# First expert of a routed layer: five residuals on the vector engine, dispatch of both batches merged and placed ahead of the next weight splits, loads issued 20 products earlier

## The chip, the core and the metric

One core of a Trainium2 chip runs the whole program. Its engines work side by side: PE multiplies matrices into PSUM (PEld is its weight load), DVE (the vector engine) and ACT (the scalar engine) do elementwise work, POOL (GpSimd) does elementwise work on SBUF and issues indirect DMAs, SP issues plain DMAs. Each engine has a list of instructions of its own and goes through it in order; an instruction that needs another engine's result waits on a semaphore, and all behind it in that list wait too. The metric is the time of one execution in microseconds (us).

## What is computed

Three stages follow each other: an attention with local windows and global tokens, a feed-forward layer with three input matrices, and a layer of eight routed experts. The change lies in the third:

```python
def _moe2_ref(x, w_gate, w1, w2, capacity) -> np.ndarray:      # x: 1088 x 512, w1: 8 x 512 x 1024, w2: 8 x 1024 x 512
    logits = x @ w_gate
    expert_idx = np.argmax(logits, axis=1)
    ...
    for i in range(N):
        e = expert_idx[i]
        if counts[e] < capacity:
            disp[e, counts[e]] = x[i]
            pos[i] = counts[e]
            counts[e] += 1
            keep[i] = True
    h = np.maximum(np.einsum('ecd,edf->ecf', disp, w1), 0.0)
    y = np.einsum('ecf,efd->ecd', h, w2)
    ...
        if keep[i]:
            out[i] = gate_w[i] * y[expert_idx[i], pos[i]]
```

The capacity is 288 rows per expert, and tokens take their places in order, batch 0 first (544 rows), then batch 1.

## The kernel before

**Matmuls in pairs of halves.** Every float32 factor is split into a rounded high part and a low part, the residual (high subtracted from the whole). A product is the sum of three: high by high, high by low, low by high. So each chunk of an expert's weights (128 x 1024 floats, 512 KB) goes through `split(j, k)`: ACT casts it to the high part, and another engine subtracts to get the residual. `residuals_on` says which engine: POOL for chunks (0, 6), (0, 7), (1, 0), (1, 1), (1, 3) and for two chunks of each later expert, else DVE. (j, k) means chunk k of the j-th expert to run; chunks 0 to 3 hold w1 (`w1h`, `w1l`), 4 to 7 hold w2 (`w2h`, `w2l`). Raw chunks lie in a ring of five buffers (`rawb`); `split` also issues on SP the load of the chunk five further on, into the buffer that it empties.

**The order by products.** The kernel writes the program's order by hand. `drive(main, sides)` steps through a main generator that yields once per matmul ("product"), and after each product runs the side generators that are due; a side yields the number of products to let pass. For the first expert (called j = 0; it holds the full 288 rows that batch 0 alone gives it) the main chain is `first_wide` (products 1 to 96: eight blocks f0 to f7 of 12 products each, one PSUM bank a block, evicted by ACT and DVE into `hhl`, the hidden activations), then `second` for rows 0 to 127 (97 to 120), for rows 128 to 255 (121 to 144) and `second_few` for the last 32 rows (145 to 160). Its sides are `final`/`finish` (routing and dispatch, below), the rows of the last feed-forward window (`tail_rows`), loads, the splits of chunks (0, 5) to (0, 7), the eight splits of expert 1 (`prepare`), and the transposes of expert 1's gathered tokens (`tokens`, tiles `xg` to `xT`).

**Routing and dispatch.** While the first expert runs, the program still has to route batch 1. `final` does: `tail_logits(3)` and `route` (on DVE: argmax, gate, one-hot rows `oh_all`; then `pp` on PE, counts by a triangular matmul; then the place of each token in its expert, and `wvr`, the rank of the experts); `columns` (five DVE instructions on 5 numbers per partition) and `rows_1` (a one-hot matrix of 5 blocks by 128) for a batch of five 128-row blocks; `values` (the other factor, 5 blocks by 24 columns by 5 values); `hand_over` (the matmuls `pd`, which scatter token numbers, output rows and gates to the expert lists); `place_rows` (the lists `idsall`) and `order` (which expert runs when). Then `start` issues three gathers of expert 1's tokens on POOL. The number of products between these steps are Y0 to Y4. Before the change, columns, rows and values run for batch 0 (blocks 0 to 4), then for batch 1 (blocks 5 to 9).

Expert 1 follows in tiles of 128 rows (`first_tile`, `second`), then experts 2, 3 and 4 of the sorted order, one tile each; the others have no rows.

Of the kernel before, what the change touches and what calls it, by code (L numbers as in the profile page):

```python
# [7 lines left out]
F32 = mybir.dt.float32  # L8
# [11 lines left out]
P = 128  # L20
# [6 lines left out]
NE = 8  # L27
# [17 lines left out]
def tile_block(ctx: ExitStack, tc: tile.TileContext, qk, qg, v, vo, vg, w123, w_out, w_gate, w1, w2, consts, out):  # L45
# [389 lines left out]
    def route(b0, b1, pool, tag, wait):  # L435
# [35 lines left out]
        pos = rt.tile([P, nb], F32, name=f"rp{b0}")  # L471
        nc.vector.tensor_reduce(pos, t, axis=AX.X, op=ALU.add)
        POS[b0] = (pos, code)
        return pp[:, nb]

    POS = {}

    def columns(b0, nb):

        pos, _ = POS[b0]  # L480
        t = rt.tile([P, 2, nb], F32, tag="pct", name="pct")
        pm = rt.tile([P, nb], BF16, tag="pcm", name="pcm")
        nc.vector.tensor_scalar(t[:, 0], pos, float(P), None, op0=ALU.is_ge)
        nc.vector.scalar_tensor_tensor(t[:, 0], pos, 2.0 * P, t[:, 0], op0=ALU.is_ge, op1=ALU.add)
        nc.vector.scalar_tensor_tensor(pm, t[:, 0], float(-P), pos, op0=ALU.mult, op1=ALU.add)

        nc.vector.tensor_scalar(t[:, 1], pos, float(CAP), NONE, op0=ALU.is_ge, op1=ALU.mult)
        nc.vector.tensor_tensor(t[:, 0], t[:, 0], t[:, 1], op=ALU.add)
        return t[:, 0], pm
# [232 lines left out]
    def tail_logits(wi):  # L722

        c0, T, x2T, pl_, logits = TAIL[wi]
        lt = XB[wi][2]
        if wi < 3:
            logits(3)
            nc.vector.tensor_copy(lt[:, :T], pl_[0:16, :T])
        yield 8
        ptl = ps_y.tile([P, 4, NE], F32, tag="py", name=f"ptl{c0}")  # L730
        for i, (c, n, row, blk) in enumerate(rows_of(wi)):
            nc.tensor.matmul(ptl[0:n, i], lhsT=lt[:, c - c0 : c - c0 + n], rhs=dup8, start=True, stop=True)
        for i, (c, n, row, blk) in enumerate(rows_of(wi)):
            nc.vector.tensor_copy(L[0:n, blk], ptl[0:n, i])
# [256 lines left out]
    def early():  # L991
# [18 lines left out]
        col, pm = columns(0, 5)  # L1010
# [3 lines left out]
        values(Bv, 0, 5, col, wv0, 3)  # L1014
        yield 44
# [78 lines left out]
    Y0, Y1, Y2, Y3, Y4 = 8, 12, 14, 14, 10  # L1094

    def final():

        yield from tail_logits(3)
        c_ = yield from route(5, 10, ps_mm, "mm", 32)
# [4 lines left out]
        sc = pB.tile([P, 512], F32, tag="hs", bufs=2, name="sc")  # L1104
        g_, p_ = (sc[:, 64 * i : 64 * i + 64].rearrange("p (a b) -> p a b", a=NE) for i in range(2))
# [183 lines left out]
```

## Time and profile before

| | before |
|---|---|
| median of 3 runs | 386.12 us (383.12 to 386.4) |
| the profiled execution | 382.62 us, of which the span from first to last instruction is 380.8 us |
| PE busy | 331.3 us (87%) |
| DVE / ACT / POOL busy | 256.2 (67%) / 178.5 (47%) / 168.6 us (44%) |
| mean DMA rate | 159 GB/s |
| mean granted TensorE clock | 0.968 of full |
| the first expert's block on PE | 252.17 to 299.74 us of the span |

The rows further down come from the profile of that one execution; times are us from the start of the span. A timeline row gives start, length (of the whole group when it ends in "xN"), engine, line, operation, output <- input, shape, and in brackets the idle time of that engine just before and what ended it. Matmul lengths overlap, so the pace of PE is read from one start to the next.

### The profile page before, as it was taken

The page shows a single profiled execution, that of the slowest core. Times are in us where ns is not written, and L with a number is a line of the kernel's source. Part 1 is how long each engine was busy: PE and PEld are TensorE (multiplying, and loading weights), DVE is VectorE, ACT ScalarE, POOL GpSimd, SP SyncE. Part 2 cuts the span into 40 slices and gives each one's busy share as a digit, 9 for nine tenths or more (in the row PEclk, how much of TensorE's full clock was granted, in tenths as well). Part 3 has the DMA queues.
Part 4 walks back from the last instruction along what each step waited for, and adds up shares of the span by engine and source line. Part 5 has one row for each costly group of instructions (what it writes and reads, how often), then busy time and mean ns, then how long its engine had stood idle before and what let it go on. Part 6 is the DMA issues. An engine that isn't in the chain of part 4 may idle for free. (4 is left out here: it accounts for less than half of the span.)

```text
span 380.8 us, 8527 instructions
## 1 busy us (share of the span) xinstructions
PE 331.3 (87%) x3115; PEld 274.3 (72%) x3115; DVE 256.2 (67%) x649; ACT 178.5 (47%) x452; POOL 168.6 (44%) x172
## 2 busy tenths in 40 slices
PE   7988789999999999966899989999249899876892
PEld 2444557777888999966799979989247688655681
DVE  2679989858782698999953385658982661566450
ACT  3876568666642323233222124535504662756640
POOL 0268686646582464574640004000935571353421
PEclk9999989999999999999999999999959999998998
DMA  7964865905297132331000237417646673398500
GB/s 270 406 246 163 297 229 205 344 26 166 74 244 157 57 100 68 112 97 69 2 0 6 107 124 275 127 58 256 197 155 200 213 283 135 95 306 279 192 22 10
DMA packets 26216, 60.67 MB, mean 159 GB/s; under 512 B 3003, under 2 KB 8123, under 8 KB 26160
## 3 DMA queue, kind: packets, MB, share of 16 engines
q1 hardware_dynamic: 24640, 55.69, 44.3%
q0 software_dynamic: 1520, 4.28, 3.1%
q8 instruction: 30, 0.49, 0.5%
q14 instruction: 26, 0.21, 0.2%
HBM read 55.61 MB, written 7.47 MB: 166 GB/s over the span
## 5 line engine op out<-in xcount | busy, mean ns | idle before, releaser
L422 PE MATMUL h<-xh,wh 128*128 128x256 f32 (+1 forms) x288 | 86.0, 299 | 8.0 <-DVE hA L408 6.8
L422 PE MATMUL h<-xl,wh 128*128 128x256 f32 (+1 forms) x288 | 85.1, 296 | 0.0
L422 PE MATMUL h<-xh,wl 128*128 128x256 f32 (+1 forms) x288 | 84.7, 294 | 0.0
L422 PEld LDWEIGHTS h<-xh,wh 128*128 128x128 f32 x288 | 55.4, 192 | 10.3 <-DVE hA L408 8.3
L422 PEld LDWEIGHTS h<-xl,wh 128*128 128x128 f32 x288 | 55.5, 193 | 0.9 <-issue 0.7
L422 PEld LDWEIGHTS h<-xh,wl 128*128 128x128 f32 x288 | 55.5, 193 | 0.3 <-issue 0.2
L412 POOL TENSOR_TENSOR hTl<-hA,hTh 128x288 fp32r<-128x288 f32 (+1 forms) x18 | 15.5, 861 | 57.1 <-ACT hTh L410 57.0
L827 DVE TENSOR_TENSOR w2l<-rawb,w2h 128x1024 fp32r<-128x1024 f32 x14 | 21.4, 1532 | 22.3 <-ACT w2h L826 22.3
L923 PE MATMUL py<-w2h,hhl 128*128 128x512 f32 x112 | 31.0, 406 | 0.2 <-ACT hhl L911 0.2
L224 POOL CAST xh<-xs 128x128 fp32r<-128x128 f32 x32 | 13.7, 428 | 36.7 <-ACT xs L222 36.7
L321 POOL TENSOR_TENSOR ct<-ct,wh 128x512 f32<-128x512 f32 x18 | 25.7, 1429 | 7.5 <-DVE ca L318 5.7
L827 POOL TENSOR_TENSOR w2l<-rawb,w2h 128x1024 fp32r<-128x1024 f32 x5 | 13.1, 2633 | 34.2 <-DVE ab L505 31.3
L702 PE MATMUL x<-hTh,wo_h 128*128 128x256 f32 (+1 forms) x96 | 28.1, 293 | 0.1
L889 PE MATMUL ph<-w1h,xT 128*128 128x512 f32 x80 | 22.2, 411 | 6.8 <-ACT w2h L826 4.3
L702 PE MATMUL x<-hTl,wo_h 128*128 128x256 f32 (+1 forms) x96 | 28.0, 292 | 0.0
L186 ACT ACTIVATE sm<-sm,nm 128x128 f32<-128x128 f32 x64 | 25.2, 399 | 5.5 <-DVE nm L181 5.4
L702 PE MATMUL x<-hTh,wo_l 128*128 128x256 f32 (+1 forms) x96 | 27.8, 289 | 0.0
L408 DVE TENSOR_TENSOR hA<-hA,h 128x256 f32<-128x256 f32 (+1 forms) x48 | 20.7, 432 | 8.5 <-PE h L422 6.8
L322 POOL TENSOR_TENSOR wl<-ct,ca 128x512 fp32r<-128x512 f32 x18 | 24.0, 1335 | 3.5 <-DVE ca L320 2.3
L923 PEld LDWEIGHTS py<-w2h,hhl 128*128 128x128 f32 x112 | 21.7, 195 | 5.3 <-ACT hhl L911 0.6
L410 ACT CAST hTh<-hA 128x256 fp32r<-128x256 f32 (+1 forms) x24 | 10.1, 419 | 32.1 <-DVE hA L408 32.1
L305 DVE TENSOR_SCALAR ca<-ca 128x512 f32<-128x512 f32 x24 | 23.5, 978 | 1.2 <-ACT ca L303 1.1
(205 smaller groups left out, 793.9 us busy)
## 6 DMA issues: line engine op xcount, KB each, us to landing
rawb<-in_w_dram SPq DMA_DIRECT2D x40, 512.0 KB, 4.3
raww<-in_w_dram SPq DMA_DIRECT2D x18, 512.0 KB, 4.5
rawv<-in_v_dram SPq DMA_DIRECT2D x16, 512.0 KB, 5.7
qk<-in_qk_dram SPq DMA_DIRECT2D x16, 320.0 KB, 6.4
rawo<-in_w_out_dram SPq DMA_DIRECT2D x6, 512.0 KB, 3.6
rw<-in_w_dram SPq DMA_DIRECT2D x5, 512.0 KB, 3.7
out_dram<-zero SPq DMA_DIRECT2D x1, 2176.0 KB, 15.9
rawg<-in_vo_dram SPq DMA_DIRECT2D x4, 512.0 KB, 6.6
```

The source lines that it names most:

```text
L186: nc.scalar.activation(sm[:, j], sm[:, j], AF.Exp, bias=nm[:, j : j + 1], scale=-1.0, accum_out=ssum[:, j : j + 1])
L224: nc.gpsimd.tensor_copy(dst[0], xs)
L305: nc.vector.tensor_scalar(a.bitcast(F32), a.bitcast(F32), F64_LO, F64_HI, op0=ALU.max, op1=ALU.min)
L321: nc.gpsimd.tensor_tensor(tf, tf, hi.bitcast(F32), op=ALU.subtract)
L322: nc.gpsimd.tensor_tensor(lo, tf, a.bitcast(F32), op=ALU.add)
L408: nc.vector.tensor_tensor(hA[:, :T], hA[:, :T], ph[:, :T], op=ALU.max)
L412: eng.tensor_tensor(hl[:, f_, c0 : c0 + T], hA[:, :T], dst.bitcast(F32), op=ALU.subtract)
L422: nc.tensor.matmul(ph[:, :T], lhsT=w_[:, a], rhs=x_[:, c, c0 : c0 + T], start=n == 0, stop=n == 11)
L702: nc.tensor.matmul(po[:, :T], lhsT=w_[:, f, d * P : (d + 1) * P], rhs=h_[:, f_, c0 : c0 + T], start=k == 0, stop=k == 17)
L827: residuals_on(j, k).tensor_tensor(l_, raw_of(j, k), h_.bitcast(F32), op=ALU.subtract)
L889: nc.tensor.matmul(ph[0:nt], lhsT=a[:, c], rhs=w_[:, c, sl], start=i == 0, stop=i == 11)
L923: nc.tensor.matmul(py[0:nt], lhsT=a[:, c, a0 : a0 + nt], rhs=w_[:, c], start=i == 0, stop=i == 23)
```

## The change

- `residuals_on`: the five residuals of the first two experts that POOL did go to DVE; those of later experts stay.
- `columns` now writes into `pos_all` and `col_all`, arrays for all ten blocks; `values` runs once over ten blocks (its five steps on twice the columns, the last one as two instructions of five blocks).
- `final`: columns and rows of batch 0 run at the very start, before batch 1's logits; `pp` comes after 24 products instead of 32; columns and rows of batch 1, then the merged values; then a long pause (44 products) up to `pd`.
- Sides: loads at product 36 instead of 56; split (0, 5) at 3 instead of 66, (0, 6) at 72, (0, 7) at 80; the splits of expert 1 at 116 to 160 instead of 85 to 158. In `early` (dispatch of the first expert alone) a pause grows from 44 to 60 products.

```diff
     def residuals_on(j, k):
-        return nc.gpsimd if (j, k) in ((0, 6), (0, 7), (1, 0), (1, 1), (1, 3)) or j > 1 and k in (2, 6) else nc.vector
+        return nc.gpsimd if j > 1 and k in (2, 6) else nc.vector
...
-    def values(Bv, b0, nb, col, wv, ncol):
+    def values(Bs, oq, nb, wv, ncol):
...
-        nc.vector.scalar_tensor_tensor(qb, q, NONE, col, op0=ALU.add, op1=ALU.add)
-        oq = rt.tile([P, 5, 3 * NE], BF16, tag="voq", name="voq")[:, 0:nb, 0:ncol]
+        nc.vector.scalar_tensor_tensor(qb, q, NONE, col_all[:, 0:nb], op0=ALU.add, op1=ALU.add)
         nc.vector.tensor_tensor(oq, iota_b[:, 0:ncol].unsqueeze(1).to_broadcast([P, nb, ncol]), qb.unsqueeze(2).to_broadcast([P, nb, ncol]), op=ALU.is_equal)
-        nc.vector.tensor_tensor(
-            Bv, oq.unsqueeze(3).to_broadcast([P, nb, ncol, NV]),
-            val_all[:, b0 : b0 + nb].unsqueeze(2).to_broadcast([P, nb, ncol, NV]), op=ALU.mult)
+        for i, Bv in enumerate(Bs):
+            b = slice(5 * i, 5 * i + 5)
+            nc.vector.tensor_tensor(
+                Bv, oq[:, b].unsqueeze(3).to_broadcast([P, 5, ncol, NV]),
+                val_all[:, b].unsqueeze(2).to_broadcast([P, 5, ncol, NV]), op=ALU.mult)
...
-    Y0, Y1, Y2, Y3, Y4 = 8, 12, 14, 14, 10
+    Y0, Y1, Y2, Y3, Y4 = 10, 12, 44, 12, 3
 
     def final():
 
+        hs_ = [pB.tile([P, 512], F32, tag="hs", bufs=2, name=f"sc{i}") for i in range(2)]
+        As = [t.bitcast(BF16)[:, 256:896].rearrange("p (b m) -> p b m", b=5) for t in hs_]
+        rows_1(As[0], columns(0, 5), 5)
         yield from tail_logits(3)
-        c_ = yield from route(5, 10, ps_mm, "mm", 32)
+        c_ = yield from route(5, 10, ps_mm, "mm", 24)
...
         yield Y0
...
-        for i in range(2):
-            col, pm = columns(5 * i, 5)
-            rows_1(As[i], pm, 5)
-            yield Y1
-            values(Bs[i], 5 * i, 5, col, wvr, 3 * NE)
-            yield Y2
+        rows_1(As[1], columns(5, 5), 5)
+        yield Y1
...
+        values(Bs, hs_[1].bitcast(BF16)[:, 0 : NBLK * 3 * NE].rearrange("p (b c) -> p b c", b=NBLK), NBLK, wvr, 3 * NE)
+        yield Y2
         pd = ps_y.tile([P, 3 * NE * NV], F32, tag="py", name="pd")
...
-            [finish(), later(6, tail_rows(3)), loads(56, (0, 6), (0, 7), (1, 0), (1, 1)), splits(0, [(5, 66), (6, 72), (7, 69)]), prepare(1, (85, 97, 112, 101, 125, 129, 135, 158)), tokens(1, (149, 154, 163))],
+            [finish(), later(6, tail_rows(3)), loads(36, (0, 6), (0, 7), (1, 0), (1, 1)), splits(0, [(5, 3), (6, 72), (7, 80)]), prepare(1, (116, 120, 124, 130, 138, 146, 152, 160)), tokens(1, (149, 154, 163))],
```

**How it moves instructions.** On POOL, at the start of the first expert's block (behind the branch), before the change; `w2l` and `w1l` are the residuals, `out_dram<-y` the scatter of a result tile, `xg<-x2d` the gathers of expert 1's tokens:

```order
L1177 COMPARE_AND_BRANCH
L827 TENSOR_TENSOR w2l_3551<-rawb,w2h_3550 128x1024 x2
L827 TENSOR_TENSOR w1l_3861<-rawb,w1h_3860 128x1024 x3
L930 DMA out_dram<-y,ids_3091 1088x512
L785 DMA xg_3544<-x2d,idsall 128x512
L785 DMA xg_3545<-x2d,idsall 128x512
L785 DMA xg_3546<-x2d,idsall 32x512
L930 DMA out_dram<-y,ids_3091 1088x512
```

and the same place after the change:

```order
L1175 COMPARE_AND_BRANCH
L785 DMA xg_3545<-x2d,idsall 128x512
L785 DMA xg_3546<-x2d,idsall 128x512
L785 DMA xg_3547<-x2d,idsall 32x512
L930 DMA out_dram<-y,ids_3093 1088x512 x2
```

POOL has no residual left in this block, and the three gathers stand ahead of both scatters.

On DVE, at the start of the same block, after the change (before the change the row behind the branch was the copy to `L`, of batch 1's logits `ptl`):

```order
L1175 COMPARE_AND_BRANCH
L482 TENSOR_SCALAR pct<-pos_all 128x5
L483 SCALAR_TENSOR_TENSOR pct<-pos_all,pct 128x5
L484 SCALAR_TENSOR_TENSOR pcm<-pct,pos_all 128x5
L486 TENSOR_SCALAR col_all<-pos_all 128x5
L487 TENSOR_TENSOR col_all<-col_all,pct 128x5
L492 TENSOR_TENSOR sc_3872<-iota_b,pcm 128x640
L827 TENSOR_TENSOR w2l_3552<-rawb,w2h_3551 128x1024
L734 COPY L<-ptl_3900 32x8
```

Columns and rows of batch 0 and the residual of chunk (0, 5) now stand in front of the routing.

On DVE, in the middle of the block, around the eviction of block f4 (rows L873 and L875 are one block's eviction of the low part of `hhl`), before the change, from batch 0's rows to f5's eviction:

```order
L493 TENSOR_TENSOR sc<-iota_b,pcm 128x640
L873 SCALAR_TENSOR_TENSOR hhl<-ph,hhl 128x256
L875 SCALAR_TENSOR_TENSOR hhl<-ph,hhl 128x32
L498 TENSOR_TENSOR vt<-oh_all,wvr 128x40
L500 TENSOR_REDUCE vq<-vt 128x5
L502 SCALAR_TENSOR_TENSOR vqb<-vq,pct 128x5
L504 TENSOR_TENSOR voq<-iota_b,vqb 128x120
L505 TENSOR_TENSOR ab_4008<-voq,val_all 128x600
L827 TENSOR_TENSOR w2l_3551<-rawb,w2h_3550 128x1024
L873 SCALAR_TENSOR_TENSOR hhl<-ph,hhl 128x256
```

and after the change, from f3's eviction to f5's:

```order
L873 SCALAR_TENSOR_TENSOR hhl<-ph,hhl 128x256
L875 SCALAR_TENSOR_TENSOR hhl<-ph,hhl 128x32
L497 TENSOR_TENSOR vt<-oh_all,wvr 128x80
L499 TENSOR_REDUCE vq<-vt 128x10
L501 SCALAR_TENSOR_TENSOR vqb<-vq,col_all 128x10
L502 TENSOR_TENSOR sc_3873<-iota_b,vqb 128x240
L505 TENSOR_TENSOR ab_4038<-sc_3873,val_all 128x600
L505 TENSOR_TENSOR ab_4039<-sc_3873,val_all 128x600
L873 SCALAR_TENSOR_TENSOR hhl<-ph,hhl 128x256
L875 SCALAR_TENSOR_TENSOR hhl<-ph,hhl 128x32
L873 SCALAR_TENSOR_TENSOR hhl<-ph,hhl 128x256
```

The merged values now stand ahead of f4's eviction, where before they stood behind it. PE's block f6 writes into the PSUM bank that f4's eviction empties: there are three banks for f0, f1, f2, f4, f5 and f6, and one of the three holds `pp` until the end of `final`.

## Rows read from the trace of the kernel before

**Rows 1.** Timeline of PE, the end of the hidden layer to the second.

```profile
263.86 1.39 PE L868 MATMUL ph<-xT,w1h 128*128 128x288 f32 x8
...
268.90 0.44 PE L511 MATMUL pd<-ab,sc 128*128 128x120 bf16 x5
280.95 0.66 PE L511 MATMUL pd<-ab,sc 128*128 128x120 bf16 x5 [11.62 <-DVE ab L505]
...
282.81 2.98 PE L923 MATMUL py<-w2h,hhl 128*128 128x512 f32 x8
285.62 1.08 PE L923 MATMUL py<-w2l,hhl 128*128 128x512 f32 x4
286.54 1.99 PE L923 MATMUL py<-w2h,hhl 128*128 128x512 f32 x8
```

**Rows 2.** Timeline of DVE in that wait, dispatch of batch 1.

```profile
267.50 1.95 DVE L483 TENSOR_SCALAR pct<-rp 128x5 f32<-128x5 f32 x1
...
277.44 1.90 DVE L498 TENSOR_TENSOR vt<-oh_all,wvr 128x40 f32<-128x40 bf16 x1
```

**Rows 3.** Timeline of POOL, residuals and the first gather.

```profile
266.02 5.70 POOL L827 TENSOR_TENSOR w2l<-rawb,w2h 128x1024 fp32r<-128x1024 f32 x2 [31.25 <-DVE ab L505]
271.68 7.60 POOL L827 TENSOR_TENSOR w1l<-rawb,w1h 128x1024 fp32r<-128x1024 f32 x3
...
289.95 1.51 POOL L785 DMA_INDIRECT xg<-x2d,idsall  x1 [0.30 <-issue]
```

**Rows 4.** Windows: busy us (instructions) of PE, PEld, DVE, ACT, POOL; clock; DMA.

```profile
278.00:281.00 3.00, 0.05 (x1) 0.04 (x1) 2.86 (x6) 0.00 (x0) 1.28 (x1) 0.50 0.47 154
```

**Rows 5.** Timeline of PE, the end of the first expert.

```profile
292.89 0.63 PE L951 MATMUL pyf<-w2h,hhl 128*64 128x512 f32 x2
...
294.80 0.66 PE L797 MATMUL xp<-cst,xg 128*128 128x128 f32 x4 [0.35 <-DMA xg<-x2d,idsall]
...
297.64 0.66 PE L797 MATMUL xp<-cst,xg 128*128 128x128 f32 x4 [1.04 <-DMA xg<-x2d,idsall]
...
299.74 1.19 PE L889 MATMUL ph<-w1h,xT 128*128 128x512 f32 x4
```

**Rows 6.** Timeline of DVE, routing and dispatch of batch 0.

```profile
254.77 0.30 DVE L734 COPY L<-ptl 32x8 f32<-32x8 f32 x3 [1.97 <-PE ptl L732]
...
259.87 0.42 DVE L873 SCALAR_TENSOR_TENSOR hhl<-ph,hhl 128x256 fp32r<-128x256 f32 x1 [1.22 <-ACT hhl L872]
...
260.37 0.20 DVE L470 TENSOR_TENSOR rt<-oh_all,pp 128x40 f32<-128x40 bf16 x1
...
262.33 0.16 DVE L483 TENSOR_SCALAR pct<-rp 128x5 f32<-128x5 f32 x1
...
263.82 0.42 DVE L873 SCALAR_TENSOR_TENSOR hhl<-ph,hhl 128x256 fp32r<-128x256 f32 x1
...
264.26 0.19 DVE L498 TENSOR_TENSOR vt<-oh_all,wvr 128x40 f32<-128x40 bf16 x1
...
265.23 0.78 DVE L505 TENSOR_TENSOR ab<-voq,val_all 128x600 bf16<-128x600 bf16 x1
265.93 1.22 DVE L827 TENSOR_TENSOR w2l<-rawb,w2h 128x1024 fp32r<-128x1024 f32 x1
```

**Rows 7.** Timeline of PE, two earlier stalls in the feed-forward layer.

```profile
166.42 0.39 PE L422 MATMUL h<-xh,wh 128*128 128x256 f32 x1 [2.10 <-DVE hA L408]
...
178.75 0.39 PE L422 MATMUL h<-xh,wh 128*128 128x256 f32 x1 [2.62 <-DVE hA L408]
```

**Rows 8.** Windows, columns as in rows 4, behind the second of these stalls.

```profile
180.00:182.00 2.00, 2.00 (x11) 2.00 (x11) 1.93 (x3) 0.16 (x1) 2.00 (x2) 0.50 0.00 0
```

**Rows 9.** Timeline of ACT, expert 1's first tile.

```profile
304.94 0.59 ACT L911 CAST hhl<-hp 128x512 fp32r<-128x512 f32 x1 [0.20 <-PE hp L910]
```

**Rows 10.** DMA issues of 255 to 300 us: KB each, median us to landing.

```profile
rawb<-in_w_dram SPq DMA_DIRECT2D x14, 512.0 KB, 4.0
...
xg<-x2d,idsall POOLq DMA_INDIRECT x5, 4.8
```

More of the change, by code (lines that the diff above doesn't have):

```diff
@@ L470, in route @@
         nc.vector.tensor_tensor(t, oh, pp[:, 0:nb], op=ALU.mult)
-        pos = rt.tile([P, nb], F32, name=f"rp{b0}")
-        nc.vector.tensor_reduce(pos, t, axis=AX.X, op=ALU.add)
-        POS[b0] = (pos, code)
+        nc.vector.tensor_reduce(pos_all[:, b0:b1], t, axis=AX.X, op=ALU.add)
         return pp[:, nb]
-    POS = {}
+    pos_all = rt.tile([P, NBLK], F32, name="pos_all")
+    col_all = rt.tile([P, NBLK], F32, name="col_all")
     def columns(b0, nb):
-        pos, _ = POS[b0]
-        t = rt.tile([P, 2, nb], F32, tag="pct", name="pct")
+        pos, col = pos_all[:, b0 : b0 + nb], col_all[:, b0 : b0 + nb]
+        t = rt.tile([P, nb], F32, tag="pct", name="pct")
         pm = rt.tile([P, nb], BF16, tag="pcm", name="pcm")
[L483 to L489, printed above, removed]
+        nc.vector.tensor_scalar(t, pos, float(P), None, op0=ALU.is_ge)
+        nc.vector.scalar_tensor_tensor(t, pos, 2.0 * P, t, op0=ALU.is_ge, op1=ALU.add)
+        nc.vector.scalar_tensor_tensor(pm, t, float(-P), pos, op0=ALU.mult, op1=ALU.add)
+        nc.vector.tensor_scalar(col, pos, float(CAP), NONE, op0=ALU.is_ge, op1=ALU.mult)
+        nc.vector.tensor_tensor(col, col, t, op=ALU.add)
+        return pm
     def rows_1(A, pm, nb):
         nc.vector.tensor_tensor(A, iota_b.unsqueeze(1).to_broadcast([P, nb, P]), pm.unsqueeze(2).to_broadcast([P, nb, P]), op=ALU.is_equal)
-    def values(Bv, b0, nb, col, wv, ncol):
-        t = rt.tile([P, nb, NE], F32, tag="rt", name="vt")
-        nc.vector.tensor_tensor(t, oh_all[:, b0 : b0 + nb], wv.unsqueeze(1).to_broadcast([P, nb, NE]), op=ALU.mult)
+    def values(Bs, oq, nb, wv, ncol):
+        t = rt.tile([P, nb, NE], F32, tag="vt", name="vt")
+        nc.vector.tensor_tensor(t, oh_all[:, 0:nb], wv.unsqueeze(1).to_broadcast([P, nb, NE]), op=ALU.mult)
         q = rt.tile([P, nb], F32, tag="vq", name="vq")
@@ L1009, in early @@
         nc.vector.tensor_scalar(wv0, mine[:, 0], -NONE, None, op0=ALU.mult)
-        col, pm = columns(0, 5)
+        pm = columns(0, 5)
         A = s2b.tile([P, 5, P], BF16, tag="pA0", bufs=1, name="pA0")
@@ L1013, in early @@
         Bv = s2b.tile([P, 5, 3, NV], BF16, tag="pB0", bufs=1, name="pB0")
-        values(Bv, 0, 5, col, wv0, 3)
-        yield 44
+        values([Bv], s2b.tile([P, 5, 3], BF16, tag="oq0", bufs=1, name="oq0"), 5, wv0, 3)
+        yield 60
         pd = ps_y.tile([P, 3 * NV], F32, tag="py", name="pd0")
@@ L1103, in final @@
             nc.vector.scalar_tensor_tensor(k_, mine[:, i], big, k_, op0=ALU.mult, op1=ALU.add)
-        sc = pB.tile([P, 512], F32, tag="hs", bufs=2, name="sc")
-        g_, p_ = (sc[:, 64 * i : 64 * i + 64].rearrange("p (a b) -> p a b", a=NE) for i in range(2))
+        g_, p_ = (hs_[0][:, 64 * i : 64 * i + 64].rearrange("p (a b) -> p a b", a=NE) for i in range(2))
         nc.vector.tensor_tensor(g_, k_.unsqueeze(1).to_broadcast([P, NE, NE]), k_.unsqueeze(2).to_broadcast([P, NE, NE]), op=ALU.is_gt)
@@ L1110, in final @@
         yield Y0
-        ab = [pB.tile([P, 512], F32, tag="y", bufs=2, name=f"ab{i}").bitcast(BF16) for i in range(2)]
-        As = [sc.bitcast(BF16)[:, 256:896].rearrange("p (b m) -> p b m", b=5), pB.tile([P, 512], F32, tag="hs", bufs=2, name="sc2").bitcast(BF16)[:, 0:640].rearrange("p (b m) -> p b m", b=5)]
-        Bs = [t[:, 0 : 5 * 3 * NE * NV].rearrange("p (b c v) -> p b c v", b=5, v=NV) for t in ab]
-        for i in range(2):
-            col, pm = columns(5 * i, 5)
-            rows_1(As[i], pm, 5)
-            yield Y1
-            values(Bs[i], 5 * i, 5, col, wvr, 3 * NE)
-            yield Y2
+        rows_1(As[1], columns(5, 5), 5)
+        yield Y1
+        Bs = [pB.tile([P, 512], F32, tag="y", bufs=2, name=f"ab{i}").bitcast(BF16)[:, 0 : 5 * 3 * NE * NV].rearrange("p (b c v) -> p b c v", b=5, v=NV) for i in range(2)]
+        values(Bs, hs_[1].bitcast(BF16)[:, 0 : NBLK * 3 * NE].rearrange("p (b c) -> p b c", b=NBLK), NBLK, wvr, 3 * NE)
+        yield Y2
         pd = ps_y.tile([P, 3 * NE * NV], F32, tag="py", name="pd")
```

## The prediction

> **What bounds the kernel now.** I read PE's timeline first. PE is the busiest engine, so time is won or lost where it stands still. In the first expert's block it does so once for long: the five matmuls of `pd` for batch 0 run at 268.90, those for batch 1 only at 280.95, after 11.62 us idle for DVE's `ab` [rows 1]. This wait is dispatch, not weights: every later matmul of this expert is queued behind `pd` in PE's order.
>
> Then DVE in that stretch. Batch 1's columns, rows and values are small instructions, but those on 5 numbers take about 2 us: six rows from 267.50 to 277.44 last 1.90 to 2.27 us [rows 2]. The same column step of batch 0 took 0.16 at 262.33 [rows 6]. What differs is POOL: it subtracts five residuals from 266.02 to 279.28, 2.5 to 2.9 us each [rows 3], and the slow steps lie wholly inside. Larger DVE steps there keep their lengths; a small step seems to be held until a POOL instruction ends.
>
> The stall costs more than its length. TensorE's granted clock is down to 0.50 (1.2 GHz) at 278 to 281 [rows 4], and after the restart eight matmuls that take 1.8 us at full pace (four take 0.92, from 285.62 to 286.54) need 2.81 [rows 1]. At full pace 285.62 would come 3.1 us after 268.90 (ten `pd` 0.6, eleven matmuls at 0.23), so at 272.0: 13.6 us lost, 11.6 stall and 2.0 slow clock. Last, the end of the first expert: from 292.89 to 299.74 there are 16 matmuls (3.65) and three groups of transposes (1.0), 4.65 us of work in 6.85 [rows 5]. PE waits for the gathered tokens: the first gather is issued at 289.95 [rows 3] and lands 4.8 us later [rows 10]. That is 2.2 us more.
>
> **What the change takes away.** With no residuals on POOL in this block, batch 1's small steps should take 0.16 to 0.2 us, and the merged values stand some 40 products ahead of `pd`. So the stall of 11.6, the slow restart of 2.0 and, because the gathers go out earlier (below), the 2.2 of token waits can all go: 15.8 us.
>
> **What it adds: DVE is late for f6.** PE's f6 needs the bank that DVE empties with f4's eviction. Before, that eviction began at 263.82 [rows 6] and f6 started about 264.4, in the middle of the eight matmuls of 263.86, hardly delayed [rows 1]. Now much DVE work stands in front:
> - At the block's start columns and rows of batch 0 take 1.49 (262.33 to 263.82, rows 6) and the residual of (0, 5) 1.14 to 1.22. DVE idled 1.97 before 254.77 [rows 6], so the copy to `L` slips by 0.7 us, by 1.2 if the branch costs DVE half a us (no row shows that). The whole routing slips with it.
> - `pp` needs f0's bank, whose eviction on DVE slips too: PE waits there 0.2 to 0.7 us at product 33. On the other hand `pp` comes eight products sooner, and DVE's idle 1.22 before 259.87 [rows 6] is used.
> - So the step after `pp`, at 260.37 before, comes at 259.5 to 259.9. From there: routing's end 1.53, f2's eviction 0.43 (together 260.37 to 262.33), columns and rows of batch 1 1.49, f3's eviction 0.44, merged values 2.5 (batch 0's took 1.67 from 264.26 to 265.93; doubled columns add about 0.1, a second 600-column step 0.70), f4's eviction 0.52. Sum 6.9: f4's bank is free at 266.4 to 266.8, against 264.3 when PE would want it.
>
> So PE stands 2.1 to 2.6 us at f6, the wait at `pp` included: I take 2.4. Nothing hides it. Behind f6 the eviction of f4 to f7 and two residuals follow on DVE, done by about 271.0, and the second layer needs the last of them some 4 us later.
>
> **The clock at f6.** A stall of 2.10 us at 166.42 was followed by matmuls at full pace; after one of 2.62 at 178.75 [rows 7] the clock was 0.50 [rows 8]. Ours lies between. A fall would cost at most the 2.0 us seen above; I leave it out of the sum, at a chance of a third.
>
> **The five residuals on DVE.** 1.14 to 1.22 each there against 2.5 on POOL. (0, 6) and (0, 7) fill DVE while PE stands or runs f6 and f7. Expert 1's eight residuals (9.8 us) run from about 272 to 289, paced by ACT's casts, which now wait behind the eviction of the first result tile (product 120, about 276.2). w1's four residuals are ready near 282, PE wants them at 286.4: covered by 4 us. What follows is expert 2's loads: each waits for a residual that frees its buffer. Chunk (2, 2) would load at about 285 and land 4.0 later [rows 10], or up to 2 later when loads queue. ACT's cast of it stands ahead of `hhl` in the first tile, at 304.94 before, 5.2 after the tile's start [rows 9]; now 291.6. So 0 to 1.2 us may be lost; I take 0.6.
>
> **The gathers.** `pd` now runs at about 270.9, the lists are ready near 272.1, and POOL issues three gathers in 1.0 to 1.5 us each [rows 3], ahead of both scatters. They land at about 278 to 281.5. PE's transposes come at products 149 to 163, from 282.8 on: covered by 4 us.
> The Trainium skill (SBUF — State Buffer, "SBUF: two separate sides") warns that POOL cannot write DMA descriptors while DVE runs certain instructions over the port that they share, and these gathers now lie beside DVE residuals. Here the gather at 289.95 ran beside two DVE residuals and took 1.51 us [rows 3]. If each took 3.6 us, the last would land 1.5 us late and the sum would be 1.5 smaller.
>
> **What moves nothing.** `loads(36)` and the pause of 60 change no row's place on any engine apart from one: chunk (1, 2) now loads ahead of the last three stores of `x2d`, on SP. It waits for the residual of (0, 5), about 256, when SP has nothing else to do but one 64 KB store. The merged arrays remove five DVE instructions, 0.2 each, counted above. All behind 299.74 keeps its order and shifts as a whole.
>
> **Sum.** 15.8 less 2.4 less 0.6 is 12.8. The profiled execution took 382.6 us, so 369.8 against it. The median of the runs is 386.1, 3.5 above that execution; the same saving gives 373.3. I predict 373.3.
>
> **Rivals.**
> - *The clock falls at f6, or the loads are late.* As forecast, but 2.0 for the clock or 1.2 to 2 for loads and gathers are lost as well: 375 to 377. For it: the 2.62 us stall. Against it: the 2.10 one.
> - *Small steps stay slow.* If not POOL's residuals but something else (the loads landing then) held DVE's small steps, batch 1's columns and values, now between 261 and 266, would be slow in front of f4's eviction: six steps by 2 us put 10 to 12 us into f6's wait, and a slow restart of 2. Time 384 to 387, no change. Against it: batch 0's same steps at 262.33 ran at 0.16 while the same loads were landing, and the slow ones begin and end with POOL's work.
> - *DVE becomes the bound (slower).* If w1's residuals of expert 1 came later than 299.7, the first tile would start later than before. They are due at 282, so 18 us would have to be added, 15 more residuals' worth of DVE, or a load that lands 18 us late. At 5 us beyond that point: 391. I see no row that leads there.
> - *More is gained.* The copy to `L` is not delayed and f6's wait is 1 us: 371.5 to 372.
>
> **How the numbers follow.** Forecast (with the gain rival) 0.68, clock or loads 0.2, small steps slow 0.07, DVE the bound 0.05. The median of before itself moved between 383.1 and 386.4, so the same saving may show as 370 or 374. Range 369 to 377.5: it takes in the clock case and the lower base, and leaves out the last two and the edges. Within 1% (about what a measurement of this kernel can tell from no change) is 382.3 to 390. Faster 0.89, same 0.07, slower 0.04.
>
> **What would show it.** In the profile after: no idle over 1 us ahead of either `pd`; DVE's 128x5 steps at 0.2; PE idle about 2.4 in f6, released by DVE's L873 or L875; expert 1's first tile at 286 to 288 instead of 299.74, and the rest as long as before. The forecast is wrong if f6's wait is over 5 us, if PE waits for `xg` or for `w1l`, or if the stretch behind the first tile grows by more than 2 us.

## The result, and the profile after

The changed kernel takes **370.69 us** (median of four runs, 369.85 to 372.31) against 384.62 us for the kernel before in the same comparison (381.53 to 386.4): ratio 0.968, 95% interval 0.963 to 0.973. It is faster by 3.2%. The profiled execution took 370.33 us against 382.62 us, so 12.3 us less; its span is 368.6 against 380.8. The forecast was 12.8 us less, and a median of 373.3 us. The page after, its first rows (busy us, share of the span, instructions of each engine):

```profile
span 368.6 us, 8523 instructions
...
PE 329.3 (89%) x3115; PEld 273.8 (74%) x3115; DVE 249.7 (68%) x650; ACT 178.5 (48%) x452; POOL 155.7 (42%) x167
```

POOL is busy 13 us less than before, and DVE 6.5 us less too, though it took five residuals over: the held small steps are gone, which had lasted 9.7 us longer than such steps do now.

PE's timeline after, from the first expert's first matmul to the second tile of expert 1. It answers [rows 1] and [rows 5]. Columns: start, length, engine, line, operation, the idle time before it and who ended it.

```profile
252.20 0.76 PE L868 MATMUL ph<-xT,w1h 128*128 128x288 f32 x4
...
266.46 0.76 PE L868 MATMUL ph<-xT,w1h 128*128 128x288 f32 x4 [1.88 <-DVE hhl L875]
...
270.43 0.70 PE L511 MATMUL pd<-ab,sc 128*128 128x120 bf16 x10
...
281.51 0.63 PE L951 MATMUL pyf<-w2h,hhl 128*64 128x512 f32 x2
...
282.90 0.60 PE L797 MATMUL xp<-cst,xg 128*128 128x128 f32 x4
...
286.54 1.20 PE L889 MATMUL ph<-w1h,xT 128*128 128x512 f32 x4
...
295.25 0.66 PE L910 MATMUL hp<-cst,hs 128*128 128x128 f32 x4 [0.84 <-ACT hs L894]
...
301.14 1.08 PE L889 MATMUL ph<-w1h,xT 128*128 128x512 f32 x4
```

The ten `pd` now run in one piece at 270.43, without the 11.62 us of idle time. The transposes of the gathered tokens (`xp`) wait for nothing. One wait is new in this block, 1.88 us in f6, ended by DVE's L875, the eviction of f4. A second, small one follows in expert 1's first tile: 0.84 us for `hs`. Expert 1's first tile starts at 286.54 instead of 299.74 [rows 5].

The places from which times are compared below are the first L868 row (f0), the first L889 row (tile 1) and the next tile's first L889 row (tile 2). What lies ahead of f0 is the same program in all kernels, but for the change's edits to `early`, and takes between 251.5 and 255.8 us in these profiles. So a stretch tells more than a span:

| kernel | median us | f0 to tile 1 | tile 1 to tile 2 | wait in f6 |
|---|---|---|---|---|
| before | 384.62 | 47.57 | 13.55 | none |
| after | 370.69 | 34.34 | 14.60 | 1.88 |

The block lost 13.23 us, the tile behind it grew by 1.05. That makes 12.2, the difference of the spans.

### The profile page after: what moved, and what is told of

Its sections match the earlier page's. It is cut to its first block, busy times and chain, and to the rows that moved or that the text cites. A ratio compares the mean times of both kernels' runs of the same rounds, so it can differ in the third digit from the quotient of the medians.

```text
span 368.6 us, 8523 instructions
## 1 busy us (share of the span) xinstructions
PE 329.3 (89%) x3115; PEld 273.8 (74%) x3115; DVE 249.7 (68%) x650; ACT 178.5 (48%) x452; POOL 155.7 (42%) x167
## 5 line engine op out<-in xcount | busy, mean ns | idle before, releaser
L827 DVE TENSOR_TENSOR w2l<-rawb,w2h 128x1024 fp32r<-128x1024 f32 x16 | 23.8, 1491 | 15.5 <-ACT w2h L826 15.5
L785 POOL DMA_INDIRECT xg<-x2d,idsall x11 | 15.0, 1363 | 43.4 <-DMA rawb<-in_w_dram 39.4
L702 PE MATMUL x<-hTh,wo_h 128*128 128x256 f32 (+1 forms) x96 | 28.9, 301 | 0.1
L702 PE MATMUL x<-hTl,wo_h 128*128 128x256 f32 (+1 forms) x96 | 28.8, 300 | 0.0
L889 PE MATMUL ph<-w1h,xT 128*128 128x512 f32 x80 | 22.3, 412 | 6.9 <-ACT w2h L826 4.3
L923 PEld LDWEIGHTS py<-w2h,hhl 128*128 128x128 f32 x112 | 20.9, 188 | 5.2 <-ACT hhl L911 0.7
## 6 DMA issues: line engine op xcount, KB each, us to landing
out_dram<-zero SPq DMA_DIRECT2D x1, 2176.0 KB, 15.2
```

The source lines that it names most:

```text
L702: nc.tensor.matmul(po[:, :T], lhsT=w_[:, f, d * P : (d + 1) * P], rhs=h_[:, f_, c0 : c0 + T], start=k == 0, stop=k == 17)
L785: nc.gpsimd.indirect_dma_start(out=xg[t], out_offset=None, in_=src, in_offset=bass.IndirectOffsetOnAxis(ap=IDS[j][0:n, t, 0:1].bitcast(I32 ...
L827: residuals_on(j, k).tensor_tensor(l_, raw_of(j, k), h_.bitcast(F32), op=ALU.subtract)
L889: nc.tensor.matmul(ph[0:nt], lhsT=a[:, c], rhs=w_[:, c, sl], start=i == 0, stop=i == 11)
L923: nc.tensor.matmul(py[0:nt], lhsT=a[:, c, a0 : a0 + nt], rhs=w_[:, c], start=i == 0, stop=i == 23)
```

## The experiments

**1. The residuals alone.** The kernel before, with one edit of the change:

```
-        return nc.gpsimd if (j, k) in ((0, 6), (0, 7), (1, 0), (1, 1), (1, 3)) or j > 1 and k in (2, 6) else nc.vector
+        return nc.gpsimd if j > 1 and k in (2, 6) else nc.vector
```

> The kernel before, with one edit of the change alone: the five residuals of POOL go to VectorE; order, dispatch and loads stay as before. Theory (POOL's subtractions hold VectorE's small steps): batch 1's steps on 128x5 take 0.16 to 0.25 us instead of 1.9 to 2.3. The wait ahead of batch 1's pd shrinks from 11.6 to 0 to 3 us and the slow restart goes; the token waits of 2.2 may stay. 9 to 13 us faster than before, ratio 0.966 to 0.977. Rival (the steps are held by something else that lies there, such as the landing loads): they stay near 2 us and the time stays within 1% of before.

Measured: 380.06 us against 384.19 us, ratio 0.990 (0.986 to 0.994); f0 to tile 1 45.09 us. The timeline of DVE in the place of [rows 2], then that of PE, then of POOL:

```profile
268.55 2.35 DVE L827 TENSOR_TENSOR w2l<-rawb,w2h 128x1024 fp32r<-128x1024 f32 x2
270.81 0.16 DVE L483 TENSOR_SCALAR pct<-rp 128x5 f32<-128x5 f32 x1
...
272.74 1.21 DVE L827 TENSOR_TENSOR w1l<-rawb,w1h 128x1024 fp32r<-128x1024 f32 x1
...
274.85 0.78 DVE L505 TENSOR_TENSOR ab<-voq,val_all 128x600 bf16<-128x600 bf16 x1
```

```profile
275.68 0.66 PE L511 MATMUL pd<-ab,sc 128*128 128x120 bf16 x5 [5.29 <-DVE ab L505]
...
293.09 0.66 PE L797 MATMUL xp<-cst,xg 128*128 128x128 f32 x4 [3.67 <-DMA xg<-x2d,idsall]
```

```profile
284.18 1.01 POOL L930 DMA_INDIRECT out_dram<-y,ids  x1 [49.79 <-ACT y L929]
285.50 2.08 POOL L785 DMA_INDIRECT xg<-x2d,idsall  x1 [0.30 <-issue]
```

The small steps are at 0.16 to 0.20 us: POOL's subtractions had held them. The landing loads, which this kernel kept, had not. But my sum for this run was wrong, 4 us gained and not 9 to 13. Two queues keep their order. On DVE three residuals (268.55 and 272.74) stand ahead of batch 1's columns and values, so `pd` still waits 5.29 us and the granted clock falls to 0.50 (274 to 280). The steps that were held before are 9.7 us shorter here, and the three residuals in front take 3.5: an estimate of 6.2 us off the wait, which fell by 6.3. On POOL the gathers stand behind the scatter of the first result tile, which cannot go before 284.18; `xp` waits 3.67 us for them. Of the change's 13.2 us in this block the edit on the residuals alone is worth 2.5. Tile 1 to tile 2 takes 13.56 us, as before, so where the rest of the 4.1 us lies this profile does not show.

**2. The order alone.** The changed kernel with the edit of experiment 1 turned back: the five residuals on POOL.

> The changed kernel with the five residuals back on POOL; the order stays the new one. Theory (POOL holds small steps, and only what lies beside its work): columns and values of batch 1 run at 261 to 266, ahead of POOL's first residual at about 267 to 268, and keep 0.16 to 0.2 us, pd finds its operands. But the small steps of place_rows at 271 (0.8 us in all) lie beside POOL's work and take about 2 us each, and the gathers stand behind POOL's residuals: they go out 3 to 8 us later and PE waits 2 to 5 us for tokens. 2 to 5 us slower than the changed kernel: 373 to 376. Rival (the order alone made the gain): 371, no token waits. Rival (moving the residuals off POOL alone made it): 381 to 386.

Measured: 376.81 us, ratio 0.980 (0.971 to 0.988); f0 to tile 1 36.02, tile 1 to tile 2 17.32. The timeline of DVE and that of POOL behind 282, then PE:

```profile
283.11 2.75 DVE L827 TENSOR_TENSOR w2l<-rawb,w2h 128x1024 fp32r<-128x1024 f32 x1 [0.59 <-ACT w2h L826]
...
285.90 3.29 DVE L827 TENSOR_TENSOR w2l<-rawb,w2h 128x1024 fp32r<-128x1024 f32 x1
```

```profile
282.32 2.46 POOL L827 TENSOR_TENSOR w1l<-rawb,w1h 128x1024 fp32r<-128x1024 f32 x1
...
284.73 3.38 POOL L827 TENSOR_TENSOR w1l<-rawb,w1h 128x1024 fp32r<-128x1024 f32 x1
```

```profile
289.85 0.43 PE L797 MATMUL xp<-cst,xg 32*128 32x32 f32 x4 [1.13 <-DVE xT L800]
...
290.73 1.68 PE L889 MATMUL ph<-w1h,xT 128*128 128x512 f32 x4 [0.46 <-issue]
```

The loss came (6.1 us in time, more than the 2 to 5 that I expected; in these two stretches 4.4), but not where I put it. The small steps of `place_rows` kept 0.2 us, since POOL's first two residuals had ended at 273.3, just ahead of them. The collision came later: four residuals of one size on two engines take turns. DVE's at 283.11 waits for POOL's of 282.32 (ends 284.78), then needs its 1.2; POOL's next starts at 284.73 and is held for 1.1 by it; DVE's next is held by that one. So DVE is late for `xT`, PE waits, and at 292 to 294, in tile 1, its clock is 0.50. Later in this tile PE waits 1.34 us for `xT` once more, behind a residual of 3.25 us on DVE. So it is not only small steps that are held, as I had read from [rows 2]. This run keeps the rest of the change as a whole; what the earlier loads or the later splits of expert 1 are worth by themselves was not run.

**3. The contention rebuilt.** In the changed kernel POOL gets four useless subtractions, started by f2's eviction, while DVE does batch 1's columns. Variants: the same work in 16 pieces (the inner loop goes by 256 instead of 1024), and eight zeroings in place of the subtractions, which read nothing (the last two lines).

```
         yield Y0
+        nc.gpsimd.tensor_copy(WS[1][1][:, 0, 0:CAP], H0[:, 2, 0:CAP].bitcast(F32))
+        for i in range(4):
+            for a in range(0, 1024, 1024):
+                nc.gpsimd.tensor_tensor(WS[1][1][:, i, a : a + 1024], WS[0][0][:, i, a : a + 1024].bitcast(F32), WS[0][1][:, i, a : a + 1024].bitcast(F32), op=ALU.subtract)
...
+        for i in range(8):
+            nc.gpsimd.memset(WS[1][1][:, i % 4].bitcast(F32), 0.0)
```

> The changed kernel, and POOL does a small copy that waits for f2's eviction and then four subtractions of 128x1024 that nobody needs, about 2.5 us each, from about 260 to 270.5. The output is not touched. Theory (a small VectorE step is held until a POOL subtraction ends): batch 1's 128x5 steps at 261 and the 128x10 steps of the values take about 2 us each, 6 to 8 of them, f4's eviction ends 7 to 10 us later, and PE waits 9 to 12 us for it in f6 instead of 1.9; 8 to 12 us slower than the changed kernel, 379 to 383. Rival (POOL's residuals were not the cause): the steps keep 0.16 us and the time stays at 371.

> As the run with four useless POOL subtractions of 128x1024, but the same work cut into sixteen pieces of 128x256, about 0.6 us each. Theory (the step waits for the POOL instruction that has begun, and gets in before the next): the steps that took 2.0 to 2.3 us take 0.4 to 0.8, f4's eviction comes 1.5 to 4 us later than in the changed kernel, the wait in f6 is 3 to 6 us instead of 9.9, and POOL's work is stretched. Rival (VectorE is slowed for as long as POOL is busy, whatever the size of its instructions): the steps still take about 2 us, f6's wait is near 10.

> As the run with useless POOL subtractions, but POOL writes zeros to 128x1024 eight times: it is as busy, and reads nothing. Theory (what they share is a way to read SBUF): VectorE's steps with two inputs from SBUF keep 0.17 us, f6's wait stays at 2 to 3 us. The Trainium skill (SBUF — State Buffer, "Who interferes with whom") says that an instruction of VectorE with two SBUF inputs contends with a POOL instruction that reads SBUF, not with one that only writes. Rival (any POOL instruction holds VectorE's small steps): they take about as long as one zeroing, some 1 us, and f6's wait grows to 5 us or more.

Measured: 379.91 us with four subtractions (ratio 0.990, 0.986 to 0.993); one execution each of the others, 378.57 in pieces and 373.26 with zeroings. DVE's timeline with four subtractions, and one line of POOL's (the first of the four):

```profile
261.57 2.00 DVE L482 TENSOR_SCALAR pct<-pos_all 128x5 f32<-128x5 f32 x1
263.61 2.29 DVE L483 SCALAR_TENSOR_TENSOR pct<-pos_all,pct 128x5 f32<-128x5 f32 x1
265.93 2.27 DVE L484 SCALAR_TENSOR_TENSOR pcm<-pct,pos_all 128x5 bf16<-128x5 f32 x1
268.12 0.16 DVE L486 TENSOR_SCALAR col_all<-pos_all 128x5 f32<-128x5 f32 x1
268.31 2.18 DVE L487 TENSOR_TENSOR col_all<-col_all,pct 128x5 f32<-128x5 f32 x1
```

```profile
261.16 2.39 POOL L1116 TENSOR_TENSOR w1l<-w1h,w1l 128x1024 fp32r<-128x1024 f32 x1
```

The pattern of [rows 2] is back, step by step, though in four steps and not in the 6 to 8 that I expected: POOL's work ended with the columns, and the steps of the values were free. The held steps end at 263.57, 265.90, 268.20 and 270.49, 2.3 us apart, as POOL's subtractions end (2.33 each). The step at 268.12 began 0.02 us ahead of POOL's fourth, and is not held. DVE's timeline with the pieces, and with the zeroings; one zeroing lasts 0.95, the first from 261.76 to 262.71:

```profile
264.08 0.66 DVE L483 SCALAR_TENSOR_TENSOR pct<-pos_all,pct 128x5 f32<-128x5 f32 x1
```

```profile
261.69 1.04 DVE L1111 TENSOR_SCALAR wvr<-rank 128x8 f32<-128x8 f32 x1
261.77 0.96 DVE L873 SCALAR_TENSOR_TENSOR hhl<-ph,hhl 128x256 fp32r<-128x256 f32 x1
...
262.20 0.55 DVE L482 TENSOR_SCALAR pct<-pos_all 128x5 f32<-128x5 f32 x1
262.84 0.17 DVE L483 SCALAR_TENSOR_TENSOR pct<-pos_all,pct 128x5 f32<-128x5 f32 x1
263.04 0.17 DVE L484 SCALAR_TENSOR_TENSOR pcm<-pct,pos_all 128x5 bf16<-128x5 f32 x1
263.12 0.54 DVE L486 TENSOR_SCALAR col_all<-pos_all 128x5 f32<-128x5 f32 x1
```

With pieces a step waits for a piece (0.58 to 0.67). With zeroings the steps with two inputs from SBUF run free, and steps with one input are held: L1111, which takes 0.17 in the changed kernel, until the first zeroing ends, and L486 until the second does. The two evictions (L873, and L875 at 262.10 with 0.63) and L482 end with L1111 or right behind it; DVE takes its steps in order, so whether L482 was held for itself these rows don't tell. The Trainium skill (SBUF — State Buffer, "Who interferes with whom") gives this rule: DVE and POOL share one pair of ports, the later one waits until the earlier instruction is over; two inputs from SBUF collide with a POOL instruction that reads, and a one-input form in a two-port mode with any. All three runs agree on who collides; that the one-input steps run in such a mode no trace shows. One row is harder to read: L1111 began 0.07 us ahead of the zeroing that it then waited for, just as POOL's copy ahead of it ended, so the start in the trace does not always tell who goes first. PE's wait in f6 in the three, four subtractions, pieces, zeroings:

```profile
274.82 1.30 PE L868 MATMUL ph<-xT,w1h 128*128 128x288 f32 x4 [9.94 <-DVE hhl L875]
```

```profile
272.11 1.30 PE L868 MATMUL ph<-xT,w1h 128*128 128x288 f32 x4 [5.10 <-DVE hhl L875]
```

```profile
268.19 0.76 PE L868 MATMUL ph<-xT,w1h 128*128 128x288 f32 x4 [2.70 <-DVE hhl L875]
```

The waits fell in the expected ranges, and the time with four subtractions too. The one execution in pieces is slower than its wait of 5.10 alone would make it: f0 began at 254.60 in it, 2.4 later than in the changed kernel, and its clock stayed low until about 277.

**4. Values behind f4's eviction.** The changed kernel with

```
-    Y0, Y1, Y2, Y3, Y4 = 10, 12, 44, 12, 3
+    Y0, Y1, Y2, Y3, Y4 = 10, 17, 39, 12, 3
```

> The changed kernel with the merged values put 5 products later, right behind f4's eviction on VectorE (pause of 17 instead of 12, the next one 39 instead of 44). Theory (f6's wait of 1.88 us is the values standing in front of f4's eviction): the wait goes, everything behind comes 1.9 us earlier, pd still finds its operands (values end near 266.5, pd at 268.5): 368.8, ratio to before about 0.963. Rival (the bank would come late anyway, or the time is lost again behind it, at expert 2's late loads or expert 1's tokens): 370 to 371.

Measured: 368.74 us, ratio 0.962 (0.954 to 0.970); f0 to tile 1 32.21, which is 2.13 less than after, tile 1 to tile 2 15.36, 0.76 more. The interval overlaps that of the changed kernel, so it is the block that tells. The wait in f6 is gone and nothing else opened in the block, so its cause is settled: the merged values stood in front of f4's eviction. What was lost again lies in tile 1. The timelines of PE, DVE and POOL there:

```profile
295.00 0.66 PE L797 MATMUL xp<-cst,xg 128*128 128x128 f32 x4 [1.59 <-DVE xT L800]
```

```profile
290.48 3.86 DVE L827 TENSOR_TENSOR w1l<-rawb,w1h 128x1024 fp32r<-128x1024 f32 x1 [0.26 <-ACT w1h L826]
```

```profile
290.85 2.40 POOL L827 TENSOR_TENSOR w1l<-rawb,w1h 128x1024 fp32r<-128x1024 f32 x1
```

Again two residuals collide, those of expert 2's chunks (2, 2) and (2, 3); DVE's takes 3.86 instead of 1.2, and ends 1.1 behind POOL's. Here too the one that waited began first by the trace, 0.37 us ahead of POOL's, while POOL still issued a gather (289.89 to 290.82). What let POOL's go ahead no run shows.

**5. Two ways on from there.** First, experiment 4 with no residual on POOL at all (the first pair of lines). Second, experiment 4 with expert 1's splits earlier (the second pair):

```
-        return nc.gpsimd if j > 1 and k in (2, 6) else nc.vector
+        return nc.vector
...
-prepare(1, (116, 120, 124, 130, 138, 146, 152, 160))
+prepare(1, (115, 116, 117, 118, 119, 138, 146, 152))
```

> The changed kernel with the values behind f4's eviction, and POOL's residuals of the later experts on VectorE too, so that POOL subtracts nothing at all. In the run with the values moved, VectorE's residual of expert 2 at 290.48 took 3.86 us beside POOL's at 290.85, and PE waited 1.59 us for xT at 295.00. Theory (the two residuals exclude each other): that residual takes 1.2 us, the 1.59 us wait goes down to under 0.9, 0.5 to 1.5 us faster than with the values moved alone: 367.2 to 368.2. Rival (VectorE then has too much to do behind 285): other waits of 1 us or more for VectorE appear in the experts' tiles, 368.5 to 371.

> The changed kernel with the values behind f4's eviction, and expert 1's first five splits asked for at products 115 to 119, ahead of the first result tile, the others at 138, 146 and 152. ScalarE's casts then fill its idle time ahead of 273 to 276. Theory (expert 2's chunks load late because expert 1's residuals free their buffers late): the loads of expert 2 start 2 us or more earlier, the wait for hs or xT in expert 1's first tile (0.84 in the changed kernel, 1.59 with the values moved) goes: 367.2 to 368.2. Rival (the loads are bound by the DMA queues, not by the buffers): they land no earlier, the wait stays, 368.5 to 369.5.

Measured: 367.12 us for the first, a little under the theory's range, ratio 0.955 (0.951 to 0.959), and 371.06 for the second, ratio 0.967 (0.964 to 0.970). The first takes back most of what tile 1 had lost: 14.41 instead of 15.36, and 14.07 in the second profile of this kernel (experiment 7). With no subtraction on POOL the residual of (2, 3) takes 1.23. The second missed both of its ranges and undid experiment 4's gain. Its loads of (1, 7) and (2, 0) and the one behind them did go out 2.5 us earlier, counted from f0, and tile 1 to tile 2 is back at 14.31; but f0 to tile 1 takes 34.14, 1.93 more than in experiment 4. ACT's timeline in it, then PE's:

```profile
281.84 1.05 ACT L826 CAST w2h<-rawb 128x1024 fp32r<-128x1024 f32 x1 [5.21 <-DMA rawb<-in_w_dram]
```

```profile
286.64 0.43 PE L797 MATMUL xp<-cst,xg 32*128 32x32 f32 x4 [1.54 <-DVE xT L800]
```

The earlier residuals sent out the loads of (1, 5) to (1, 7) and (2, 0) one after the other, beside the gathers. The one gather whose landing the trace gives took 7.9 us from issue (3.1 to 5.4 in experiment 4), and the cast of a chunk of `w2` waited 5.21 us for its load. Behind it in ACT's queue stand the second result tile and the casts to `xT`, so PE waited 1.54. So the theory's loads came earlier, and the rival's queues took more than that back; how much of it is the gathers beside the loads was not tried.

**6. The split of (0, 5).** The changed kernel with this split at product 66 again, as before the change.

```
-splits(0, [(5, 3), (6, 72), (7, 80)])
+splits(0, [(5, 66), (6, 72), (7, 80)])
```

> The changed kernel with the split of chunk (0, 5) asked for at product 66 again, as before the change, instead of 3. Theory (f6 waits because VectorE has more work than time ahead of f4's eviction, the residual of (0, 5) at 254.24 among it): the copy to L, the routing and f4's eviction come 0.6 to 1.2 us earlier, f6's wait is 0.7 to 1.3 us instead of 1.88, the time 0.5 to 1.2 us shorter than that of the changed kernel: 369.5 to 370.2. Rival (what the copy to L gains is taken back where VectorE waits for f2's or f3's matmuls, or the residual at 66 delays the second layer): 370.5 to 372.

Measured: 370.87 us, ratio 0.968 (0.964 to 0.973), f0 to tile 1 34.28: no change. The timelines of DVE and of PE:

```profile
260.13 0.20 DVE L470 TENSOR_TENSOR rt<-oh_all,pp 128x40 f32<-128x40 bf16 x1 [0.66 <-PE pp L468]
```

```profile
267.25 0.76 PE L868 MATMUL ph<-xT,w1h 128*128 128x288 f32 x4 [1.99 <-DVE hhl L875]
```

DVE was earlier with the routing, and then idle for 0.66 until PE reached `pp`. The step behind `pp` comes 7.14 us behind f0, as in the changed kernel (259.34 there). So the late copy to `L` is not on the path to f6; that path begins at `pp`, whose place is a product number.

**7. Side by side.** The changed kernel and the better one of experiment 5 on one chip, five rounds.

> The changed kernel once more, beside the next one: 370 to 371.

> The changed kernel with the values behind f4's eviction and no residual on POOL at all, once more, so that it stands beside the changed kernel on the same chip. Theory (f6's wait of 1.9 and the collision of residuals in expert 1's first tile are both gone): 2.5 to 4 us faster than the changed kernel, 366 to 368, and no wait above 1 us in the first expert's block. Rival (its lead came from the other chip or from the first 250 us, which differ from run to run): within 1.5 us of the changed kernel.

Measured: 370.98 us (ratio 0.968, 0.964 to 0.973) and 367.26 us (0.957, 0.953 to 0.961): 3.7 us apart, 1.0%. Their blocks from f0 to tile 1 take 34.30 and 32.22 us, tile 1 to tile 2 14.24 and 14.07. PE in the better one:

```profile
293.34 0.66 PE L910 MATMUL hp<-cst,hs 128*128 128x128 f32 x4 [0.20 <-issue]
```

No wait above 0.3 us is left in these stretches. This kernel beats the changed one and the one before. The two stretches give 2.25 of the 3.7 us. The profiles don't show the rest: behind tile 2 this kernel's took 68.46 us and the changed kernel's 65.77, with waits of 3.55 and 2.25 us ahead of a later expert's first matmuls; in all thirteen profiles that last stretch lies between 65.8 and 68.5, whatever the kernel.

## Why the prediction was right, and where it was off

**The time: forecast 373.3, measured 370.69.** The sum was a little too large (12.8 us; 12.2 between the two profiled executions), and yet the time came out 2.6 us below the forecast. The base explains 1.5 of this: the kernel before took 386.12 us when I added up, and 384.62 in the comparison. The other 1.1 is the saving between the medians, 13.9. It moves with the runs: side by side in experiment 7 the changed kernel was 12.6 us faster than the kernel before. That the time lies in the range rests on the sum; that it came out so low rests on the base and is luck.

**The stall, the restart and the tokens: forecast 15.8, measured 15.2.** From the first `pd` to `pyf` the kernel before took 23.99 us (268.90 to 292.89); after takes 11.08 (270.43 to 281.51) with two products more in it, 0.47 at 0.233 each, so 10.61 for the same work. The difference of 13.38 is the stall of 11.62 and 1.76 of slow clock, where I had 2.0. From `pyf` to tile 1 before took 6.85, after 5.03: the token waits were 1.82, where I had 2.2. The term was too large because I had worked out the waitless stretch as 4.65 from matmul lengths.

**The cause of the stall.** That POOL's subtractions hold DVE's steps, and the landing loads do not, is shown by experiments 1 and 3. One step was misread: "Larger DVE steps there keep their lengths". The evictions kept theirs; they take one input from PSUM, not two from SBUF. The 128x640 step started between two of POOL's instructions. Experiment 2 has a 128x1024 residual held for twice its length. And the kernel before had shown it on POOL's side, in the first of the residuals of [rows 3] by itself and in the last:

```profile
266.02 3.40 POOL L827 TENSOR_TENSOR w2l<-rawb,w2h 128x1024 fp32r<-128x1024 f32 x1 [31.25 <-DVE ab L505]
276.28 3.00 POOL L827 TENSOR_TENSOR w1l<-rawb,w1h 128x1024 fp32r<-128x1024 f32 x1
```

Beside them DVE had a residual (265.93 to 267.15, [rows 6]) and the 128x640 step (276.27 to 277.08); the one at 271.68, with nothing large beside it, took 2.34. The mean of 2.5 to 2.9 us in the prediction had hidden this. Two of its counts were off as well: five steps between 267.50 and 277.44 were held, not six (the one at 273.97 took 0.16), and the merged arrays removed four DVE instructions, not five. Nothing in the sum hung on this, but it hid what experiments 4 and 5 found: the collision goes on in later experts, where the change left residuals on POOL.

**The wait in f6: forecast 2.4, measured 1.88.** DVE's timeline after, at the places that the prediction named:

```profile
255.37 0.29 DVE L734 COPY L<-ptl 32x8 f32<-32x8 f32 x3
...
261.30 0.16 DVE L482 TENSOR_SCALAR pct<-pos_all 128x5 f32<-128x5 f32 x1
...
264.40 1.48 DVE L505 TENSOR_TENSOR ab<-sc,val_all 128x600 bf16<-128x600 bf16 x2
265.80 0.42 DVE L873 SCALAR_TENSOR_TENSOR hhl<-ph,hhl 128x256 fp32r<-128x256 f32 x1
266.13 0.18 DVE L875 SCALAR_TENSOR_TENSOR hhl<-ph,hhl 128x32 fp32r<-128x32 f32 x1
```

The copy to `L` came 0.60 late, as forecast (0.7), the small steps took 0.16, and f4's bank was free at 266.31, just below the 266.4 to 266.8 of the forecast, because the step after `pp` came at 259.34 and not at 259.5 to 259.9. The wait at `pp` that I put into the 2.4 (0.2 to 0.7) did not show. Experiment 4 shows that the order on DVE is the cause, experiment 6 that the late copy is not.

**The clock.** It stayed up. The window after that wait, columns as in [rows 4]:

```profile
266.00:268.00 2.00, 1.54 (x12) 1.57 (x12) 2.00 (x6) 0.91 (x1) 0.00 (x0) 1.00 0.68 279
```

The granted clock is 1.00, as it was behind the 2.10 us wait of [rows 7]. That I left the 2.0 us out of the sum was right, but between one wait of 2.10 and one of 2.62 us it was a bet, and I had given the fall a third.

**The gathers.** `pd` at 270.43 (forecast 270.9), and POOL's timeline after:

```profile
272.57 1.02 POOL L785 DMA_INDIRECT xg<-x2d,idsall  x1 [39.41 <-DMA rawb<-in_w_dram]
273.90 1.41 POOL L785 DMA_INDIRECT xg<-x2d,idsall  x1 [0.30 <-issue]
```

They took 1.02 and 1.41 us, the third, at 275.61, 0.92, and `xp` waited for nothing. The case in which each takes 3.6 us did not come in this kernel.

**The late loads: forecast 0.6, measured 1.05.** ACT waited for a load, as forecast, but for chunk (2, 3) and not (2, 2). That this load was late because a residual freed its buffer late is argued from the program's order. ACT's timeline after:

```profile
293.65 1.05 ACT L826 CAST w1h<-rawb 128x1024 fp32r<-128x1024 f32 x1 [1.32 <-DMA rawb<-in_w_dram]
294.61 0.59 ACT L894 ACTIVATE hs<-ph 128x512 f32<-128x512 f32 x1
```

The cast stands ahead of `hs`, for which PE waited 0.84. The size of this term moves: in the second profile of the same kernel tile 1 took 14.24 us, 0.69 above before, and not 14.60.

**The sum.** 15.2 less 2.0 (the wait in f6 with its restart) is 13.2, less 1.05 is 12.2; the forecast was 15.8 less 2.4 less 0.6. The errors are 0.6 us or less each and partly cancel, which is luck.

## What to carry to other kernels

Before work goes from one engine to another, look at what the other engines do to each other while it runs there: where DVE and POOL both read two operands from SBUF here, they worked one after the other, and a 0.16 us step cost a whole instruction of its neighbour. Taking the contention away was worth little while the queue's order keeps the late work late, and the better order alone still collides further on: here each edit alone gave 2.5 and 11.6 us of the 13.2 in this block, and of the 11.6 the next tile took 3.8 back. And when work is moved forward, ask whose buffer the engine was about to free: five products later for the values were worth 2 us.

## What the runs showed of the hardware

- A DVE step with its inputs from SBUF and a POOL subtraction excluded each other at every size that ran: 0.16 us became 1.9 to 2.3 (the one-input L482 among them, 2.00), 1.2 became 2.75 to 3.86, and POOL's 2.35 became 3.38. With residuals queued on both engines they took turns. DVE's evictions, which read PSUM, kept 0.41 and 0.18 beside POOL's subtractions.
- POOL's zeroing held one-input steps of DVE (0.54 and 1.04 us instead of 0.17) and left two-input steps alone (0.17). Evictions behind a held step ended with it, so they show 0.96 and 0.63.
- Waits of PE of 1.88, 1.98 and 1.99 us in f6 left its clock at 1.00; behind the 2.70 us of the zeroings it was 0.56 at 269 to 271, and behind the 2.62 us of [rows 7] 0.50. The length of a wait alone does not tell: in experiment 2 the clock fell to 0.50 behind waits of 1.13 and 0.46 close together, and in the second kernel of experiment 5 it stayed at 1.00 behind 1.54 and 0.45.
- In one run, where 512 KB loads went out beside gathers, a gather's landing took 7.9 us (3.1 to 5.4 in experiment 4) and a cast waited 5.21 for its load.
- One gather of experiment 2, issued at 292.15, took 3.40 us where others took 0.92 to 2.1; DVE subtracted residuals at 292.11, 293.44 and 295.24 beside it. What held it was not tried.
